# Attention and two gated layers on one core: merging the key halves of the last 64 queries later, a TensorE turn for the first rows, and moved conversions

## The chip, the core and the metric

The kernel runs on one core of one Trainium2 chip. The metric is the time of one execution on the device in microseconds; three executions of the kernel before took 1224.55 to 1224.67, median 1224.65. The profile is of one more execution, and it gives times from the first to the last instruction of that one (its span).

## What is computed

```python
# attention: 4 batches x 8 heads, 1152 keys, head size 64
q_pool = q.reshape(B, H, S // 2, 2, D).mean(axis=3)       # 576 queries
scores = scale * matmul(q_pool, k.T)
scores = scores - max(scores, axis=-1)                     # row maximum
attn = exp(scores); attn = attn / (sum(attn, -1) + 1e-9)
x = attn @ v                      # laid out as 2304 tokens x 512
# two layers, each: h = x @ w_in (512x2048); g = gate(h); x = g @ w_out
# gates: h - tanh(h), then h * sigmoid(1.702 h)
```

## The kernel before, in words

**Attention.** Two heads make a pair; there are 16 pairs, and the two heads of a pair lie in partitions 0 to 63 and 64 to 127 ("sides"). Each pair has two stages, h = 2p and 2p + 1, one for each half of its 576 queries (288 each); so h runs from 0 to 31. A stage computes nine key blocks of scores, transposed (128 keys in the partitions, 288 queries along the free axis): `scores` (L348) issues four steps of two matmuls into one PSUM tile, three for the product in split precision (L355, L356) and a last one, `sel` by `row` (L356), that adds the negated row maximum. ScalarE takes the exponential (L362); POOL adds up key blocks for the row sums (L373). At the stage's end `products` (L381) multiplies by v (L388), sums by ones (L397), and ScalarE copies the result out (L405; L411 for the last pair, tiles `u` and `us`).

**Row maxima** have to be known before the scores of their stage. `unit(p, n)` (L289) computes a piece of the untransposed scores into a PSUM tile `mx` and reduces it on VectorE (L316) into two columns of `mt`. Units 0 to 5 are three 128-query blocks by two 512-key blocks, unit 6 is the last 128 keys for four query blocks, 7 and 8 are the fourth query block. Units 9 and 10, the corners, are the last 64 queries (QL): their matmuls (L311) put the first half of the keys' scores in partitions 0 to 63 and the second half's in 64 to 127, so that one reduction handles both. `max_rows` (L318) merges columns of `mt`: part 0 for the first 384 queries (L324), part 1 for the rest; part 1 also merges the corner's two chunks (L327) and, with a `tensor_tensor` that reads partitions 64 to 127 beside 0 to 63, its two key halves (L328). `send_rows` (L331) transposes 32 by 32 blocks on VectorE (L335) and writes the pieces into `row` with small DMAs (L342), on SP's queue (SPq).

**Order.** Everything is scheduled by hand. All tiles of the attention in PSUM (`mx`, `sc`, `acc`, `warm`) share four buffers in turn; a tile's first matmul waits until the reader of the tile four before is done. The strings `usual` and `begin` (L457, L458) give each stage's order: S is a block of scores, X, C and R are units (own units 7 to 10 or 9 and 10 first, then units of the next pair). A usual even stage does units 9 and 10 of its own pair and 0 to 3 of the next; a usual odd stage does 4 to 8. Part 1 is merged and sent right after unit 10, inside the even stage; part 0 after unit 6, inside the odd stage (L570 to L575). Around the products, jobs are run at four places: "start", "load", "pre" and "gp" (ahead of the products in program order) and "end" (behind them). An engine runs its instructions strictly in this order, so a "pre" job on ScalarE comes behind the last exponential and before the copy of `acc`, and an "end" job behind that copy.

Such jobs are: the preparation of later pairs (L258 to L287, `ql` at L274 on VectorE, `kl` at L287 on POOL), the normalisation of the pair before (`sums`, `recip`, `spread`, `normalise`, L413 to L446), the first eight pieces of the weights (`piece`, L169: a load on SP, then shift, sign, flush, tail and split, L127 to L156, on ScalarE, VectorE and POOL), and `split_x` (L103) of the first token block: a ScalarE copy (L106) and a VectorE subtraction (L107) for each of four heads' pairs. The pieces take one step per stage from h = 2 (`slots_at`, L479) and the rest in h = 30 and 31; `split_x` runs at the "end" of h = 20, 22, 24 and 26 (L489).

**The opening** (L512 to L553): loads, then units 0 to 6 of pair 0 with idle matmuls (`keep_warm`, L514, L517) between them, `max_rows` and `send_rows` of part 0 (three of the six DMAs on ScalarE's queue), 15 pairs of idle matmuls, and then stage 0.

**The layers** (`moe`, L587) follow: 40 jobs of two steps, each the first product (L613, two PSUM tiles `h`), the gate on ScalarE, VectorE and POOL, and two steps later the second product (L708, four PSUM tiles `y`). Its PSUM and SBUF pools are laid where the attention's were. The first token block was split in the attention; the second is split at its first "start" (L755 to L758), ahead of the first gate in ScalarE's order.

## Time and profile before

| | |
|---|---|
| median of three runs | 1224.65 us (1224.55 to 1224.67) |
| the profiled execution's own time | 1224.87 us |
| its span, first to last instruction | 1223.1 us |
| TensorE matmuls (PE) busy | 1199.9 us, 98% |
| weight loads (PEld) busy | 980.5 us, 80% |
| VectorE (DVE) busy | 903.2 us, 74% |
| ScalarE (ACT) busy | 623.0 us, 51% |
| GpSimd (POOL) busy | 481.4 us, 39% |
| granted TensorE clock | 1.000 of full speed (2.4 GHz) |
| attention, up to the first matmul of the layers | 423.24 us |

The attention fills the first third of the span and the layers the rest. Matmuls overlap and their ends are modelled, so that the shares of PE tell little by themselves: what a stage costs is read from the distance between the starts of its products and those of the stage before. A chain of waits is followed back from the end of its stretch: every piece in it either released the next one or stood right ahead of it on its engine. Square brackets in a row of the timeline give the idle time of the engine before the row and what ended it.

### The profile page before, as it was taken

The numbers are of one execution on the slowest core, as the hardware profiler recorded it, in microseconds if no ns is written. First come the engines' busy times: TensorE is split into PE (matmuls) and PEld (weight loads), VectorE is DVE, ScalarE is ACT, GpSimd is POOL, SyncE is SP. The second block draws the span as 40 slices with busy tenths as digits, with TensorE's granted clock in tenths as the row PEclk, the third lists the DMA queues.
The fourth block names the chain that finished last, engine by engine and source line by source line (L and its number), as shares of the span: only waits on it lengthen the run. The fifth ranks groups of instructions, "written<-read, shape, count | busy, mean of one in ns | idle before, by whom it ended". The sixth has DMA issues, their size and how long they took to land.

```text
span 1223.1 us, 23096 instructions
## 1 busy us (share of the span) xinstructions
PE 1199.9 (98%) x9484; PEld 980.5 (80%) x9484; DVE 903.2 (74%) x1053; ACT 623.0 (51%) x914; POOL 481.4 (39%) x325
## 2 busy tenths in 40 slices
PE   9999999999999999999999999999999999999998
PEld 7777767676667787898898898898888888888887
DVE  6688887887678599999999999999545645554333
ACT  3565656565455487666656656656433222322211
POOL 5687887877777523333233323232100101100000
PEclk9999999999999999999999999999999999999999
DMA  3322232223321111111101011111111111110011
GB/s 122 117 75 87 91 125 97 84 74 102 113 87 41 30 45 35 53 52 53 35 35 53 35 50 38 35 43 61 52 36 52 35 52 35 52 35 18 27 59 71
DMA packets 30506, 73.09 MB, mean 60 GB/s; under 512 B 11200, under 2 KB 11712, under 8 KB 30400
## 3 DMA queue, kind: packets, MB, share of 16 engines
q1 hardware_dynamic: 30376, 71.61, 17.1%
q8 instruction: 74, 1.21, 0.4%
q14 instruction: 32, 0.26, 0.1%
q10 hardware_dynamic: 24, 0.00, 0.0%
HBM read 66.58 MB, written 4.79 MB: 58 GB/s over the span
## 4 chain that ended last, share of the span: by engine, by line
PE 73%; DVE 17%; ACT 6%; issue 2%; POOL 2%; DMA 0%; SPq 0%; DVEq 0%; POOLq 0%; ACTq 0%
PE y L708 24%; PE h L613 22%; PE acc L388 11%; PE sc L359 9%; DVE mt L316 4%; PE acc L397 3%; PE mx L304 3%; DVE gg L671 2%; DVE gg L654 2%; ACT u L652 2%; DVE wt L134 2%; ACT a L673 1%; DVE xb L728 1%; DVE m L328 1%; DVE wt L128 1%
## 5 line engine op out<-in xcount | busy, mean ns | idle before, releaser
L316 DVE TENSOR_REDUCE mt<-mx 128x2 fp32r<-128x1024 f32 (+2 forms) x176 | 194.8, 1133 | 69.0 <-PE mx L304 44.4
L613 PE MATMUL h<-hl,big 128*128 128x512 f32 (+1 forms) x940 | 211.6, 377 | 0.0
L156 POOL TENSOR_TENSOR big<-wt,big 128x512 fp32r<-128x512 f32 x46 | 61.0, 1327 | 364.7 <-ACT big L155 364.7
L613 PEld LDWEIGHTS h<-hl,big 128*128 128x128 f32 x940 | 174.0, 188 | 28.6
L362 ACT ACTIVATE pf<-sc 128x576 f32<-128x576 f32 x288 | 173.9, 653 | 42.4 <-PE sc L359 32.8
L373 POOL TENSOR_TENSOR sum<-sum,pf 128x576 f32<-128x576 f32 x126 | 183.7, 1458 | 9.9
L708 PE MATMUL y<-g,big 128*128 128x512 f32 (+1 forms) x780 | 185.3, 368 | 0.7 <-POOL g L625 0.6
L708 PE MATMUL y<-big,g 128*128 128x512 f32 x702 | 181.0, 390 | 0.0
L708 PEld LDWEIGHTS y<-g,big 128*128 128x128 f32 x780 | 142.7, 188 | 20.7 <-POOL g L625 2.3
L708 PEld LDWEIGHTS y<-big,g 128*128 128x128 f32 x702 | 131.6, 188 | 27.1
L623 ACT ACTIVATE g<-gg 128x1024 fp32r<-128x1024 f32 (+1 forms) x80 | 77.9, 974 | 137.9 <-DVE gg L684 78.2
L388 PE MATMUL acc<-pf,v 128*32 128x288 f32 x2304 | 146.3, 407 | 0.3 <-DVE mt L316 0.3
L728 DVE TENSOR_TENSOR xb<-xb,y 128x512 f32<-128x512 f32 (+1 forms) x114 | 72.2, 655 | 86.8 <-PE y L708 86.8
L613 PE MATMUL h<-hl,w 128*128 128x512 f32 (+1 forms) x564 | 127.0, 377 | 0.9 <-ACT e L667 0.9
L388 PEld LDWEIGHTS acc<-pf,v 128*32 128x32 f32 x2304 | 71.6, 110 | 65.9 <-ACT pf L362 4.3
L613 PEld LDWEIGHTS h<-hl,w 128*128 128x128 f32 x564 | 104.3, 188 | 18.3 <-ACT e L667 1.2
L625 POOL TENSOR_TENSOR g<-gg,g 128x1024 fp32r<-128x1024 f32 (+1 forms) x39 | 87.3, 2238 | 62.0 <-ACT g L623 62.0
L673 ACT ACTIVATE a<-u 128x1024 f32<-128x1024 f32 (+1 forms) x40 | 39.1, 977 | 131.7 <-DVE gg L671 131.7
L680 ACT ACTIVATE a<-h 128x1024 f32<-128x1024 f32 (+1 forms) x40 | 37.6, 941 | 117.4 <-PE h L613 117.4
L359 PE MATMUL sc<-qh,kh 64*128 64x288 f32 x576 | 91.5, 314 | 4.3 <-DVE mt L316 4.3
L359 PE MATMUL sc<-row,sel 64*128 64x288 f32 x576 | 85.3, 291 | 0.4 <-DMA row<-tt 0.4
L625 DVE TENSOR_TENSOR g<-gg,g 128x1024 fp32r<-128x1024 f32 (+1 forms) x41 | 48.9, 1193 | 49.6 <-ACT g L623 49.6
(91 smaller groups left out, 2051.7 us busy)
## 6 DMA issues: line engine op xcount, KB each, us to landing
raw<-in_moe_w_in_dram SPq DMA_DIRECT2D x32, 512.0 KB
raw<-in_moe_w_out_dram SPq DMA_DIRECT2D x32, 512.0 KB
v<-in_v_dram SPq DMA_DIRECT2D x16, 576.0 KB
kr<-in_k_dram SPq DMA_DIRECT2D x15, 576.0 KB
qr<-in_q_dram SPq DMA_DIRECT2D x15, 576.0 KB
rbd<-rd SPq DMA_DIRECT2D x32, 144.0 KB
out_dram<-xb SPq DMA_DIRECT2D x18, 256.0 KB
row<-tt SPq DMA_DIRECT2D x125, 0.5 KB
```

The source lines that it names most:

```text
L156: nc.gpsimd.tensor_tensor(lo, t, f32(hi), op=ALU.subtract)
L316: nc.vector.tensor_reduce(out, src, AX.X, ALU.max, negate=True)
L359: nc.tensor.matmul(sc[:, s, 0:HB], w[r], m[r, xs], start=(n == 0), stop=(n == 3))
L362: nc.scalar.activation(pf, sc[:, :, 0:HB], AF.Exp, scale=SCALE)
L373: nc.gpsimd.tensor_add(out, parts[p, x], new)
L388: nc.tensor.matmul(acc[32 * n:32 * n + 32, 0], pairs[p]["v"][:, s, t, 32 * h:32 * h + 32], new[t][:, s, :], start=(t == 0), stop=(t == KT ...
L613: nc.tensor.matmul(hb[:, j, 0:TBS[b]], wi[:, c, w, :], x[r][c], start=(k == 0), stop=(k == 3 * NKC - 1))
L623: nc.scalar.activation(gt[:, :, 0, :], g, AF.Copy)
L625: eng.tensor_tensor(gt[:, :, 1, :], g, f32(gt[:, :, 0, :]), op=ALU.subtract)
L673: nc.scalar.activation(a, u, AF.Relu, bias=-T2)
L708: nc.tensor.matmul(ys[m][:, 0:w], lhsT, rhs, start=(fp == 0 and not low and j == p == 0), stop=(fp == 1 and low and j == 1))
L728: nc.vector.tensor_add(dst, dst, ys[m][:, 0:w])
```

## The change

Corners: the corner units write into columns of `mt` beside the others, so that one reduction makes the four results of part 1, and L327 and L328 go. The two key halves, which lie in different partitions, are no longer merged there: all 128 values of a side are sent, into a new tile `cr`, and a VectorE reduction `end_rows` over the two halves writes the last 64 columns of `row`, behind the products of the even stage in program order and ahead of its "end" jobs. Part 0 of pair 0 no longer goes through transposes and DMAs: `first_rows` turns it with six small matmuls against an identity, and one ScalarE copy writes `row`. Before it, the first three steps of stage 0's first two score blocks are issued; 4 pairs of idle matmuls stand in place of 15. The orders of the first two stages change: one unit (index 2 of pair 1) goes from stage 0 to stage 1. The steps of the weights' pieces are all done by h = 30 with their last split at the "pre" of h = 31; h = 20, 24 and 28 take two steps each. `split_x` goes to the "pre" of h = 10, 12, 14 and 16. `us` is put in a pool that outlives the attention, and `y`'s PSUM pool is made before `h`'s.

```diff
         nil = fixed("nil", 128)
         sel = ap.tile([128, 128], F32R, name="sel")
...
-        mts = [[fixed(f"{nm}{i}", 32) for nm in ("mt", "m2", "m3")] for i in range(2)]
+        m2, ident = spare[0][:, 0:384], spare[1][:, 0:64]
+        nc.vector.memset(f32(m2), 0.0)
+        mts = [[fixed(f"{nm}{i}", 32) for nm in ("mt", "m3")] for i in range(2)]
+        crs = [ap.tile([128, 2 * QL], F32R, name=f"cr{i}") for i in range(2)]
...
+            nc.gpsimd.memset(f32(ident), 0.0)
+            for r in sides:
+                nc.gpsimd.affine_select(
+                    out=ident[r], in_=f32(ident[r]), compare_op=ALU.not_equal, fill=1.0, base=0,
+                    pattern=[[-1, 64]], channel_multiplier=1)
+            for mt, _ in mts:
+                nc.gpsimd.memset(f32(mt[:, 28:30]), 3.0e38)
...
-            for t in rows:
+            for t in rows + crs:
                 nc.gpsimd.memset(f32(t[:]), 0.0)
...
         def new_pair(p):
-            mt, m2, m3 = mts[p % 2]
-            pairs[p] = dict(mt=mt, m2=m2, m3=m3, cq=corners[p % 2], row=rows[p % 2], twos=[])
+            mt, m3 = mts[p % 2]
+            pairs[p] = dict(mt=mt, m3=m3, cq=corners[p % 2], row=rows[p % 2],
+                cr=crs[p % 2], twos=[])
...
-                out = d["mt"][:, 16:24].rearrange("p (j s) -> p j s", j=4)
+                out = d["mt"][:, 20:28].rearrange("p (j s) -> p j s", j=4)
...
-                out, src = d["mt"][:, 8 * c + 2 * j:8 * c + 2 * j + 2], mx
+                out, src = d["mt"][:, 10 * c + 2 * j:10 * c + 2 * j + 2], mx
...
-                out, src = d["mt"][:, 24 + 2 * a:26 + 2 * a], mx[:, :, 0:HB]
+                out, src = d["mt"][:, 8 + 10 * a:10 + 10 * a], mx[:, :, 0:HB]
             nc.vector.tensor_reduce(out, src, AX.X, ALU.max, negate=True)
 
-        def max_rows(p, part):
+        def max_rows(p, part, out=None):
             d = pairs[p]
-            n = 6 if part == 0 else 2
-            at = 0 if part == 0 else 6
-            m = d["m2"] if part == 0 else d["m3"]
-            mt = f32(d["mt"][:, 0:24]).rearrange("p (c j) -> p j c", c=3)
-            nc.vector.tensor_reduce(m[:, 0:n], mt[:, at:at + n, :], AX.X, ALU.min)
-            if part == 1:
-                c = f32(d["mt"][:, 24:28]).rearrange("p (a s) -> p s a", a=2)
-                nc.vector.tensor_reduce(m[:, 2:4], c, AX.X, ALU.min)
-                nc.vector.tensor_tensor(
-                    m[0:64, 2:4], f32(m[0:64, 2:4]), f32(m[64:128, 2:4]), op=ALU.min)
+            mt = f32(d["mt"][:, 0:30]).rearrange("p (c j) -> p j c", c=3)
+            at, n = (0, 6) if part == 0 else (6, 4)
+            out = d["m3"][:, at:at + n] if out is None else out
+            nc.vector.tensor_reduce(out, mt[:, at:at + n, :], AX.X, ALU.min)
...
         def send_rows(p, part):
             d = pairs[p]
-            m = d["m2"] if part == 0 else d["m3"]
             tt = ap.tile([128, 32], F32R, tag="tt", name="tt", bufs=2)
-            nc.vector.transpose(f32(tt[:]), f32(m[:]))
-            for c in range(6 - 2 * part):
+            nc.vector.transpose(f32(tt[:]), f32(d["m3"][:]))
+            for c in range(6 * part, 6 + 4 * part):
                 j, s = divmod(c, 2)
-                q0 = 384 * part + 128 * j
-                w = min(128, SP - q0)
-                row = f32(d["row"][64 * s:64 * s + 1, q0:q0 + w])
-                queue = nc.scalar if p == part == 0 and c % 2 else nc.sync
-                queue.dma_start(
-                    out=row.rearrange("o (a i) -> o a i", i=32),
-                    in_=f32(tt[c:c + 32 * (w // 32 - 1) + 1:32, :]))
+                row = f32((d["row"] if j < 4 else d["cr"])[:])
+                q0 = 128 * j if j < 4 else 0
+                nc.sync.dma_start(
+                    out=row[64 * s:64 * s + 1, q0:q0 + 128].rearrange("o (a i) -> o a i", i=32),
+                    in_=f32(tt[c:c + 97:32, :]))
+
+        def end_rows(p):
+            d = pairs[p]
+            nc.vector.tensor_reduce(
+                d["row"][:, 512:], f32(d["cr"][:]).rearrange("p (h i) -> p i h", h=2),
+                AX.X, ALU.min)
+
+        def first_rows():
+            max_rows(0, 0, m2[:, ::64])
+            rp = ps.tile([128, 2, 512], F32, tag="ps", name="rp")
+            for j in range(3):
+                for a, r in enumerate(sides):
+                    nc.tensor.matmul(
+                        rp[:, a, 64 * j:64 * j + 64], m2[r, 128 * j:128 * j + 128], ident[r],
+                        start=True, stop=True)
+            nc.scalar.activation(
+                pairs[0]["row"][:, 0:384].rearrange("p (j a i) -> p a j i", j=3, a=2),
+                rp[:, :, 0:192].rearrange("p a (j i) -> p a j i", j=3), AF.Copy)
...
-        def scores(g):
+        opened = {}
+
+        def scores(g, some=slice(0, 4)):
             p, i = divmod(g, 2 * KT)
             x, t = divmod(i, KT)
             d = pairs[p]
-            sc = ps.tile([128, 2, 512], F32, tag="ps", name="sc")
+            sc = opened.pop(g, None)
+            if sc is None:
+                sc = ps.tile([128, 2, 512], F32, tag="ps", name="sc")
+            else:
+                some = slice(3, 4)
             ks, xs = slice(128 * t, 128 * t + 128), slice(HB * x, HB * x + HB)
             steps = (
                 (d["kh"][:, ks], d["qh"]), (d["kl"][:, ks], d["qh"]),
                 (d["kh"][:, ks], d["ql"]), (sel, d["row"]))
-            for n, (w, m) in enumerate(steps):
+            for n, (w, m) in list(enumerate(steps))[some]:
                 for s, r in enumerate(sides):
                     nc.tensor.matmul(
                         sc[:, s, 0:HB], w[r], m[r, xs], start=(n == 0), stop=(n == 3))
+            if some.stop < 4:
+                opened[g] = sc
+                return
             pf = ap.tile([128, 2, HB], F32, tag="pf", name="pf", bufs=10)
             nc.scalar.activation(pf, sc[:, :, 0:HB], AF.Exp, scale=SCALE)
             probs[g] = pf
...
-                        wpool.tile([128, SP], F32, name="u"), ap.tile([128, SP], F32, name="us"))
+                        wpool.tile([128, SP], F32, name="u"), wpool.tile([128, SP], F32, name="us"))
...
         usual = "S C S C S S X S S S X S S X X", "S X S S S X S R S S S X S X"
-        begin = "S X S X S C S C S S S S X S X X", "S X S X S X S R S S S S X S X"
+        begin = "S X S S S X S C S S S C S X X", "S X S S S X S S X S X S S R X X"
...
-        slots_at = [h for h in range(2, NH) for _ in range(1 if h < NH - 2 else 3)]
+        slots_at = [h for h in range(2, NH - 1) for _ in range(2 if h in (20, 24, 28) else 1)]
         for n, (kind, f) in enumerate(order):
             ld, shift, *more, split = piece(kind, f)
             mine = slots_at[4 * n:4 * n + 4]
             at(mine[0], "pre", shift)
             for h, job in zip(mine[1:], more, strict=True):
                 at(h, "end", job)
-            at(min(mine[-1] + 1, NH - 1), "pre" if mine[-1] < NH - 1 else "end", split)
+            at(mine[-1] + 1, "pre", split)
         for c in range(NKC):
-            at(NH - 12 + 2 * c, "end", split_x, 0, [c], nc.vector)
+            at(10 + 2 * c, "pre", split_x, 0, [c], nc.vector)
...
-        warm = [ps.tile([128, 2, 512], F32, tag="ps", name="warm") for _ in range(3)][-1]
+        warm = ps.tile([128, 2, 512], F32, tag="ps", name="warm")
...
         for n in range(7):
             unit(0, n)
             keep_warm(4)
-        max_rows(0, 0)
-        send_rows(0, 0)
-        keep_warm(15)
+        for g in range(2):
+            scores(g, slice(0, 3))
+        keep_warm(2)
+        first_rows()
+        keep_warm(2)
...
             products(p, x)
+            if x == 0:
+                end_rows(p)
             do(h, "end")
...
         mp = ctx.enter_context(tc.tile_pool(name="moe", bufs=1))
+        ps_y = ctx.enter_context(tc.tile_pool(name="ps_y", bufs=4, space=PSUM))
         ps_h = ctx.enter_context(tc.tile_pool(name="ps_h", bufs=2, space=PSUM))
-        ps_y = ctx.enter_context(tc.tile_pool(name="ps_y", bufs=4, space=PSUM))
```

## Rows read from the trace of the kernel before

**Rows 1.** Stages: us; busy PE, PEld, DVE, ACT, POOL; clock, DMA share, GB/s

```profile
239.62:252.68 13.06, 12.45 (x180) 8.84 (x184) 11.34 (x14) 8.31 (x15) 10.05 (x8) 1.00 0.17 46
252.68:264.65 11.97, 11.97 (x180) 8.78 (x184) 8.96 (x12) 6.89 (x14) 10.84 (x8) 1.00 0.46 172
277.71:290.90 13.19, 12.13 (x180) 8.74 (x184) 8.90 (x13) 5.93 (x13) 10.47 (x8) 1.00 0.45 157
...
560.00:1100.00 540.00, 538.27 (x2538) 465.54 (x2537) 407.92 (x473) 263.74 (x342) 115.41 (x70) 1.00 0.12 43
```

**Rows 2.** Chain of waits, stages 18 to 21: start us, us, what

```profile
247.74 0.14 DVE m L327
...
247.90 1.06 DVE m L328
...
250.36 0.50 PE mx L304 x2
250.86 1.06 PE sc L359 x16
...
260.71 0.23 PE mx L304 x2
...
283.90 0.42 ACT big L106
```

**Rows 3.** VectorE's lines L328, L335, L274: duration in ns, least, median, most

```profile
L328 DVE TENSOR_TENSOR m<-m x16: 246/1054/1059, 23.7 to 403.0; 64x2 fp32r<-64x2 f32 x16
...
L335 DVE STREAM_TRANSPOSE tt<-m x32: 211/211/214, 15.2 to 404.1; 128x32 f32<-128x32 f32 x32
...
L274 DVE TENSOR_TENSOR ql<-qs,qh x15: 697/1499/1960, 28.4 to 385.8; 128x576 fp32r<-128x576 f32 x15
```

**Rows 4.** Timeline of POOL, stage 18

```profile
247.51 1.43 POOL L373 TENSOR_TENSOR sum<-pf 128x576 f32<-128x576 f32 x1 [2.62 <-ACT pf L362]
```

**Rows 5.** Timeline of TensorE, stages 18 and 19

```profile
247.81 0.39 PE L304 MATMUL mx<-kh,qh 64*128 64x512 f32 x2
...
249.49 0.29 PE L359 MATMUL sc<-row,sel 64*128 64x288 f32 x2
...
258.71 0.40 PE L304 MATMUL mx<-kh,qh 64*128 64x512 f32 x2
```

**Rows 6.** Timeline of VectorE, stages 18 and 19

```profile
254.47 0.77 DVE L128 TENSOR_SCALAR wt<-raw 128x512 int32<-128x512 int32 x1
...
259.16 1.23 DVE L316 TENSOR_REDUCE mt<-mx 128x2 fp32r<-128x1024 f32 x1 [2.16 <-PE mx L304]
```

**Rows 7.** Chain of waits, the opening and stages 0 and 1

```profile
14.99 0.18 DVE m L324
...
16.87 1.70 DMA row<-tt
...
18.71 0.70 PE sc L359 x2
...
26.28 4.57 PE acc L388 x72
...
39.30 4.50 PE acc L388 x72
```

**Rows 8.** Timeline of SP's queue, stage 1 (six of L342)

```profile
38.03 3.22 SPq L342 DMA_DIRECT2D row<-tt  x6
```

**Rows 9.** Timeline of TensorE, stages 30 and 31 and the layers' first steps

```profile
410.77 0.43 PE L397 MATMUL acc<-sum,ones 128*32 128x288 f32 x1 [0.61 <-POOL sum L373]
...
423.24 4.45 PE L613 MATMUL h<-big,w 128*128 128x384 f32 x24 [0.83 <-ACT us L411]
...
432.72 5.70 PE L613 MATMUL h<-hl,w 128*128 128x512 f32 x24 [0.86 <-ACT e L667]
```

**Rows 10.** Chain of waits where the layers begin

```profile
425.02 1.86 DMA s<-us
...
427.07 2.20 ACT hl L106 x4
```

## The prediction

> **What bounds the kernel now.** I read the table of stages first. From 560 to 1100 us PE is busy for 538.27 of 540 us at clock 1.00 [rows 1]: the layers run at TensorE's pace, so what the attention or the turn to the layers gains moves the layers forward as a block and reaches the end. In the attention a usual even stage takes 13.06 us and the odd one behind it 11.97, though PE is never idle in the odd one and the even one has nearly the same work, two corner units in place of unit 6 [rows 1]. The same 13.06 stands in all 14 even stages from 2 to 28; the odd stages 21, 23, 25 and 27 take 13.19 instead of 11.97, of which PE sits idle for 1.06 [rows 1].
>
> The chain of waits says why. In the even stage it leaves PE, goes through VectorE's merging of the corners (L327 0.14 us, L328 1.06) and comes back to PE at 250.36, when a reduction has freed a PSUM buffer [rows 2]. PE's last matmul ahead of that starts at 249.49 and takes 0.13 to the next, so PE stood from 249.62 to 250.36 [rows 2, 5]. L328 works on 64 by 2 values, and its least time is 246 ns, its median 1054 [rows 3]. It begins at 247.90 and ends at 248.96; POOL's addition runs from 247.51 to 248.94 [rows 2, 4]. So most of L328 is a wait for POOL's instruction to end.
>
> In the slow odd stages the chain goes through ScalarE's `split_x` copy, which stands between the copy of `acc` and the next exponentials [rows 2].
>
> **The change, part by part.** Durations and the sum are those of the profiled execution: 1224.87 us, 1223.1 of it span, 0.22 above the median of the runs.
>
> *Corners, even stages 2 to 28.* L327 and L328 go: 0.14 + 1.06 and two hand-overs of 0.02 to 0.04, about 1.25 us on VectorE ahead of the transpose. The following reduction is then limited by its matmul: TensorE issues it at 247.81, and in the odd stage such a reduction starts 0.45 after its matmul (258.71 to 259.16) and takes 1.23, so the buffer is free at 247.81 + 0.45 + 1.23 = 249.49 [rows 5, 6]. PE wants it at 249.62: that wait goes. Late next is the last unit's buffer: freed at 249.62 + 0.45 + 1.23 = 251.30, wanted, after two units of 0.23 and 1.06 of scores, at 251.14 [rows 2]. A wait of 0.16 stays, and a restart (0.50 for a unit's two matmuls behind a wait, in place of 0.23 [rows 2]): products at 251.80 instead of 252.68, 0.88 earlier. Without that wait, with a unit's 0.39 [rows 5], it is 251.14 + 0.39 = 251.53, 1.15 earlier. The bounds are these two. I take 0.95, near the replay with the wait, since its two times are only 0.16 apart: 14 x 0.95 = **13.3 us**.
>
> *What takes their place.* `end_rows` is a reduction of 128 by 128 values: between L327 (4 values, 0.14) and a unit (1024, 1.23) that is about 0.27 [rows 2, 6]. It lies behind the units on VectorE, where 2.16 us are idle before the next stage's first reduction [rows 6]; its cost is nothing while that holds, 0.27 a stage if it doesn't. It adds a wait for four DMAs. The transpose is done at about 248.0, SP issues four DMAs at 3.22 / 6 = 0.54 each, and the last lands 1.70 later, at 251.9 [rows 7, 8]. VectorE comes to it after its last unit and L128, at some 254. Behind it stand `recip`, `ql` and the next stage's reductions, with that same idle time. The corners' DMAs are four as before, 128 values each for 64.
>
> *`split_x`* leaves the "end" of stages 20 to 26: 4 x (13.19 - 11.97) = **4.9 us**. At the "pre" of 10 to 16 ScalarE's copy (0.42) lies in the products' 4.5 us, when ScalarE waits for `acc`. The subtraction is a VectorE instruction with two inputs; `ql` of that kind takes 0.70 to 1.96 here [rows 3], and POOL is busy beside it. I take nothing: its cover is the 2.16 us, and without that an odd stage would lose what it loses now. The Trainium skill (SBUF — State Buffer, Who interferes with whom) says that a VectorE instruction with two SBUF inputs and a GpSimd one that reads SBUF exclude each other for a whole instruction, while a reduction never contends. L328 agrees with it. By that rule the moved subtraction can block, or be blocked, each time: it is the third rival below.
>
> *Weights' steps.* From 30 and 31 they go to 20, 24 and 28, a second VectorE step each, of 0.70 to 1.96 by the nearest kind of row [rows 3], in the same idle time: nothing, or at worst 3 x 0.9 where the stage already has `ql` and a shift. The pieces' loads come up to two stages earlier on SP, past loads of q, k and v; each needs a buffer whose last reader runs three stages before, so SP isn't held. In stage 30 PE waits 0.61 for POOL's sums [rows 9], which ran against three of these steps on VectorE: **0.6 us**, or nothing.
>
> *The opening.* Part 0's reduction ends at 15.17 and the first `row` step starts at 18.71 [rows 7]: 3.54 us of transpose, DMA issue and 1.70 of landing. New: six 64-column matmuls, at most three pairs of 0.39 [rows 5], I take 0.4; PE's queue ahead of them (two opened blocks, two idle pairs) ends, as I put it, near 15.6; a ScalarE copy of 384 columns, 0.42 as L106 [rows 2], with hand-overs: `row` is there at 16.6, 2.1 earlier. From there the old stage took 26.28 - 18.71 = 7.57 to its products. It now has six steps of scores less and one unit less, and VectorE's reductions are spread. PE's work is seven blocks of 0.53, two last steps and six units of 0.23 to 0.27, some 5.5 us [rows 2]; with small waits for buffers I take 5.9. First products at 22.5 in place of 26.28: **3.8 us**, bounds 2.1 (the row alone) and 4.3. POOL's new constants and VectorE's memset fall where both wait for the first loads. The granted clock is 1.000 over the whole span, the present pauses of the opening included, and the new ones (about 0.2 us ahead of the `row` step) are shorter; so 22 idle matmuls less cost nothing.
>
> *Stage 1* now holds seven units: 11.97 + 0.23 and the usual small waits, 12.4, against 13.02 [rows 7]: 0.6 less. But unit 6 comes late, so the transpose ends 1.1 after the products start; six DMAs (3.22) and 1.70 of landing [rows 7, 8] make it 6.05 after, and stage 2 wants `row` at 5.9: 0.3 lost with the restart. **0.3 us**, bounds -1 and +1.
>
> *The turn.* `split_x` of the second block starts on ScalarE at 427.07, behind the DMA that reads `us` (425.02 + 1.86); the first gate follows it, and the third product begins at 432.72 after 0.86 of idle PE [rows 9, 10]. With `us` out of the attention's memory and the last split gone from ScalarE's queue, the copies start near 423.2 and end at 425.4, before the first product does (about 427.6, where its 4.45 end). The gate then starts when the first product ends, near 427.6, instead of 429.27, and releases the third product 1.7 earlier, at 431.0; PE is ready at 432.72 - 0.86 = 431.86: **0.9 us**. The order of the PSUM pools could save the 0.83 ahead of the first product too [rows 9]; the trace doesn't show which buffer the last `acc` holds, so that is only in the bounds.
>
> **Sum:** 13.3 + 4.9 + 0.6 + 3.8 + 0.3 + 0.9 = 23.8 us off 1224.87: **1201.1 us**.
>
> **Rivals.** *(1) Backlog on VectorE.* The even stages become shorter and VectorE keeps `end_rows`, `ql` and the conversions in a smaller gap, so that the odd stage gives half back. Against it: the 0.27 of `end_rows` and the 0.3 by which the reductions end later against the products leave 1.6 of the 2.16 us. For it: `ql`'s spread to 1.96. 14 x 0.5 returned: 1208. *(2) POOL too late.* It is busy for 10.05 + 10.84 of the 25.03 us of a pair [rows 1], of 24.1 then, and its additions must fall between the exponentials and the ones-matmuls. If 0.3 a pair is lost: 1205.3. *(3) `split_x` costs the same where it is put*, if the moved subtraction waits for POOL's instruction as L328 does, or POOL for it: 4.9 back, 1206. *(4) The opening stays bound by VectorE's reductions*, with only the row's 2.1 gained or less: 1203.5. *(5) The wait moves on*: the transpose meets POOL's instruction in L328's place, and the 13.3 us go: 1214.5. Against it: 32 transposes of 211 to 214 ns, whatever POOL did [rows 3]. *(6) Slower.* `end_rows` waits for its DMAs at the head of VectorE's queue and every even stage's reductions behind it stand. To lose the 23.8 us, 15 stages must each lose 1.6 beyond the idle time: the DMAs would have to land at about 259.7, 9 us after their issue, not 1.70. Price from there: each further microsecond costs 15 us, 1240 at one.
>
> **Chances.** The forecast 0.54; (1) 0.13, (2) 0.08, (3) 0.07, (4) 0.08, (5) 0.05, (6) 0.03, and 0.02 for a gain within 0.2%, which is about what a measurement here tells from no change. Low end: the bounds (0.2 more in each of 14 stages, 0.8 at the first product, 0.5 at the opening, 0.7 in stage 1) together give 1196.3. High end: 1209 takes in (1) to (4). Faster 0.95, same 0.02, slower 0.03.
>
> **What would show it.** Right: even stages of about 12.1, odd ones of 12.0 throughout, no VectorE instruction of the corner chain above 0.25 us, first products near 22.5, the third product of the layers right behind the second, the layers' own length unchanged. Wrong: PE waiting in odd stages for a reduction (1) or for POOL in the ones-matmuls (2); stages 11 to 17 longer than 12 (3); idle VectorE before `end_rows`, released by a DMA (6). The forecast falls as a whole if even stages stay at 13.06 with L328 gone.

## The result, and the profile after

The changed kernel takes 1205.66 us, the median of four runs (1205.05 to 1205.94), beside 1224.60 for the kernel before: a ratio of 0.9845 [0.9828, 0.9862]. That is 18.9 us, where 23.5 were forecast from the median; the time lies inside the range. The profiled execution took 1205.63 us, 1203.8 of it span, at a clock of 1.00.

The table of stages of the changed kernel shows stages 16 to 19, and a stretch of the layers (us; busy PE, PEld, DVE, ACT, POOL; clock, DMA share, GB/s):

```profile
205.70:217.92 12.22, 12.19 (x179) 8.80 (x177) 10.37 (x12) 8.32 (x15) 9.28 (x7) 1.00 0.04 4
217.92:230.84 12.92, 12.25 (x178) 8.81 (x176) 12.08 (x14) 6.18 (x13) 10.89 (x9) 1.00 0.43 161
230.84:243.07 12.23, 12.20 (x179) 8.80 (x177) 9.72 (x12) 8.32 (x15) 8.30 (x6) 1.00 0.18 47
243.07:255.06 11.99, 11.99 (x179) 8.80 (x177) 9.79 (x13) 6.87 (x14) 11.62 (x9) 1.00 0.49 174
541.90:1081.90 540.00, 538.16 (x2538) 465.52 (x2537) 408.10 (x472) 263.75 (x342) 115.50 (x70) 1.00 0.13 43
```

Against [rows 1] the even stages went from 13.06 to 12.22 or 12.23, with PE idle for 0.03 of that by the modelled ends of its matmuls, and the layers run as before. Stage 17, the second row, takes 12.92 instead of 11.98, with PE idle for 0.67. TensorE's timeline of stage 18 shows a wait that is left in the even stages:

```profile
240.91 0.40 PE L315 MATMUL mx<-kh,qh 64*128 64x512 f32 x2
241.16 0.29 PE L385 MATMUL sc<-qh,kh 64*128 64x288 f32 x2
...
242.21 0.93 PE L315 MATMUL mx<-kh,qh 64*128 64x512 f32 x4
243.07 4.57 PE L417 MATMUL acc<-pf,v 128*32 128x288 f32 x72
```

A unit in the middle of the stage takes 0.25 to the start of the next matmul (240.91 to 241.16); the last two take 0.86 to the products, as in the kernel before (0.84). The chain of waits has the last unit start at 242.64, 0.43 behind the one ahead of it, when a VectorE reduction frees its buffer. Matmuls overlap, so the idle time hides most of this.

VectorE's timeline shows the end of stage 16, the part of stage 17 ahead of PE's idle 0.67, and stage 30:

```profile
213.85 0.17 DVE L334 TENSOR_REDUCE m<-mt 128x4 fp32r<-128x12 f32 x1
214.06 0.21 DVE L339 STREAM_TRANSPOSE tt<-m 128x32 f32<-128x32 f32 x1
...
219.77 1.74 DVE L107 TENSOR_TENSOR big<-xb,big 128x384 fp32r<-128x384 f32 x1
221.43 0.28 DVE L350 TENSOR_REDUCE row<-cr 128x64 fp32r<-128x128 f32 x1
221.63 1.71 DVE L141 SCALAR_TENSOR_TENSOR wt<-wa,wt 128x512 f32<-128x512 f32 x1
...
223.60 1.91 DVE L285 TENSOR_TENSOR ql<-qs,qh 128x576 fp32r<-128x576 f32 x1
225.43 1.21 DVE L327 TENSOR_REDUCE mt<-mx 128x2 fp32r<-128x1024 f32 x1
...
388.95 0.29 DVE L350 TENSOR_REDUCE row<-cr 128x64 fp32r<-128x128 f32 x1 [3.45 <-DMA cr<-tt]
```

POOL's timeline over the same stretch of stages 16 and 17:

```profile
216.68 4.42 POOL L402 TENSOR_TENSOR sum<-sum,pf 128x576 f32<-128x576 f32 x3
221.05 1.74 POOL L298 TENSOR_TENSOR kl<-kr,kh 128x576 fp32r<-128x576 f32 x1
223.45 1.44 POOL L274 TENSOR_TENSOR qs<-qr 128x576 f32<-128x576 f32 x1 [0.66 <-DVE r L455]
```

Merge and transpose now follow each other directly; the 1.06 of [rows 2] is gone. But `split_x`'s subtraction (L107) takes 1.74 us, and it ends 0.41 after POOL's `sum` (219.77 + 1.74 = 221.51; 221.10). The flush behind it (L141) takes 1.71 and ends 0.55 after POOL's `kl` (223.34; 222.79). `ql` takes 1.91. Then the next stage's first reduction starts late, and PE waits.

The chain of waits of the opening stands against [rows 7]:

```profile
13.74 1.44 POOL qs L274
...
15.20 0.68 ACT qh L278
15.89 0.39 ACT row L362
...
16.32 0.40 PE sc L385 x2
...
22.40 4.50 PE acc L417 x72
```

The `row` step starts at 16.32 instead of 18.71, and stage 0's products at 22.33 (the first record of them; the chain has 22.40) instead of 26.28. The copy of `row` stood behind `qh` of pair 1 on ScalarE, which waits for POOL's `qs`; by the trace the turning matmuls were done at 15.44.

TensorE's timeline at the end of stage 30 and in the turn, against [rows 9]:

```profile
392.66 0.43 PE L426 MATMUL acc<-sum,ones 128*32 128x288 f32 x1 [0.44 <-POOL sum L402]
...
405.13 4.43 PE L646 MATMUL h<-big,w 128*128 128x384 f32 x24 [0.83 <-ACT us L440]
409.40 4.32 PE L646 MATMUL h<-big 128*128 128x384 f32 x24
413.56 5.64 PE L646 MATMUL h<-hl,w 128*128 128x512 f32 x24
```

The third product comes right behind the second, 8.43 after the first instead of 9.48. The wait of 0.83 ahead of the first is as it was.

### The profile page after: what moved, and what is told of

Same layout as the page of the kernel before. It is cut to its first block, busy times and chain, and to the rows that moved or that the text cites. A ratio compares the mean times of both kernels' runs of the same rounds, so it can differ in the third digit from the quotient of the medians.

```text
span 1203.8 us, 23024 instructions
## 1 busy us (share of the span) xinstructions
PE 1192.8 (99%) x9468; PEld 977.5 (81%) x9468; DVE 910.0 (76%) x1035; ACT 623.9 (52%) x915; POOL 484.2 (40%) x332
## 3 DMA queue, kind: packets, MB, share of 16 engines
q8 instruction: 74, 1.21, 0.4%
## 4 chain that ended last, share of the span: by engine, by line
PE 73%; DVE 16%; ACT 7%; POOL 2%; issue 2%; DMA 1%; DVEq 0%; SPq 0%; ACTq 0%; POOLq 0%
PE y L741 23%; PE h L646 22%; PE sc L385 13%; PE acc L417 10%; DVE gg L704 3%; PE mx L315 3%; PE acc L426 2%; DVE gg L687 2%; ACT u L685 2%; DVE wt L134 2%; ACT a L706 2%; DVE wt L141 1%; DVE wt L128 1%; DVE xb L761 1%; DVE wt L148 1%
## 5 line engine op out<-in xcount | busy, mean ns | idle before, releaser
L327 DVE TENSOR_REDUCE mt<-mx 128x2 fp32r<-128x1024 f32 (+2 forms) x176 | 195.6, 1136 | 54.2 <-PE mx L315 30.5
```

Of the source, the lines that this page charges most:

```text
L327: nc.vector.tensor_reduce(out, src, AX.X, ALU.max, negate=True)
```

## The experiments

The experiments are called e1 to e12. Every kernel changes the one after, except e3, which changes the one before. Ratios are to the kernel before. Unless said otherwise each computes everything.

**The corners' merge put back (e1).**

```diff
+            if part == 1:
+                m = d["m3"]
+                nc.vector.tensor_tensor(
+                    m[0:64, 8:10], f32(m[0:64, 8:10]), f32(m[64:128, 8:10]), op=ALU.min)
...
-                row = f32((d["row"] if j < 4 else d["cr"])[:])
...
-            if x == 0:
-                end_rows(p)
```

> The changed kernel with the merge of the corners' two key halves put back between the reduction and the transpose (64 by 2 values, two inputs); cr and end_rows go, all else stays. Theory (that instruction waits for POOL's first addition to end, holds the reductions behind it, and so the PSUM buffers): it takes 1.05 us in the even stages 2 to 28, these take 12.9 to 13.1 us again instead of 12.23, and the kernel 1205.7 + 14 x 0.8 = 1216 to 1218. Rival (the gain comes from elsewhere, L327 or the corners' column order): it takes 0.25, the even stages stay within 0.2 of 12.23, 1206 to 1208.

1214.11 us, 0.9914 [0.9899, 0.9929]. The merge instruction (least, median, most ns), and a usual even stage in the table of stages:

```profile
L337 DVE TENSOR_TENSOR m<-m x16: 158/1043/1047, 22.6 to 394.1; 64x2 fp32r<-64x2 f32 x16
```

```profile
235.51:248.56 13.05, 12.44 (x178) 8.83 (x176) 11.27 (x13) 8.30 (x15) 10.01 (x8) 1.00 0.17 45
```

The even stages are back at 13.05 to 13.06. The loss is less than 14 of their gains, because the odd stages from 11 to 17 went to 11.97 to 12.03 and stage 29 to 11.98: beside longer even stages the late `ql` harms nothing, though `split_x`'s subtraction still takes 0.89 to 1.63.

**`split_x` in stage 31 (e2).**

```diff
-            at(10 + 2 * c, "pre", split_x, 0, [c], nc.vector)
+            at(NH - 1, "pre", split_x, 0, [c], nc.vector)
```

> The changed kernel with all four split_x steps of the first block at the pre of stage 31 instead of one each at 10, 12, 14 and 16. Theory (in stages 10 to 16 the moved subtraction and the steps behind it wait for POOL's instructions on VectorE and hold the next stage's first reduction): stages 11, 13, 15 and 17 go from 12.24, 12.65, 12.24 and 12.92 to 12.0, 2.1 us in all, and stage 31 has room on ScalarE (4 x 0.42 in the products' 4.5 us) and VectorE: 1203.5. Rival (those odd stages are long for another reason, such as the conversions' steps there): they stay long, 1205.5 or, with a later turn, more.

1204.08 us, 0.9833 [0.9818, 0.9847], 1.6 under the changed kernel. Stages 11, 13, 15 and 17 take 11.97 to 11.99. The subtraction of `split_x` (first four of eight in the attention), in the changed kernel:

```profile
L107 DVE TENSOR_TENSOR big<-xb,big x8: 542/1096/1741, 147.5 to 774.1; 128x384 fp32r<-128x384 f32 x8
```

and with all four in stage 31:

```profile
L107 DVE TENSOR_TENSOR big<-xb,big x8: 545/554/1637, 399.7 to 772.4; 128x384 fp32r<-128x384 f32 x8
```

It is 0.55 alone and up to 1.74 beside POOL. Stage 22 was 0.63 too long in this execution, so that not all of the 2.1 shows.

**POOL's additions one block later, in the kernel before (e3).** The sum starts with blocks 1 and 2 and takes block 0 last (pairs 1 to 14); nothing else is changed.

```diff
-            new = probs[(2 * p + x) * KT + t]
-            if t == 0:
-                parts[p, x] = new
...
+            if t < 2:
+                return
+            blocks = [probs[(2 * p + x) * KT + i] for i in range(t + 1)]
+            if t == 2:
+                parts[p, x] = ap.tile([128, 2, HB], F32, tag="sum", name="sum")
+                nc.gpsimd.tensor_add(parts[p, x], blocks[1], blocks[2])
+                return
+            nc.gpsimd.tensor_add(parts[p, x], parts[p, x], blocks[t])
+            if t == KADD - 1:
+                nc.gpsimd.tensor_add(parts[p, x], parts[p, x], blocks[0])
```

> The kernel before with one thing changed: for pairs 1 to 14 POOL's five additions of a stage start with blocks 1 and 2 and take block 0 last, so that the first one begins about 0.65 us later, behind the third exponential instead of the second. The number of additions is the same. Theory (L328 is long only because it meets POOL's first addition): it takes 0.25 us where it took 1.05, the even stages 4 to 28 fall from 13.06 to about 12.3, and the kernel from 1224.6 to 1214 to 1216, the merge still in its place. Rival (L328 is long by itself, or it meets some other instruction of POOL): it stays at 1.05 and the kernel at 1224 or above.

1221.75 us, 0.9977 [0.9967, 0.9986]. The old merge instruction:

```profile
L328 DVE TENSOR_TENSOR m<-m x16: 156/156/1016, 23.5 to 399.5; 64x2 fp32r<-64x2 f32 x16
```

The table of stages, 22 and 23:

```profile
282.85:295.07 12.22, 12.18 (x179) 8.80 (x177) 9.86 (x14) 8.31 (x15) 7.49 (x6) 1.00 0.14 45
295.07:312.09 17.02, 13.69 (x178) 10.30 (x176) 11.10 (x13) 7.19 (x15) 13.95 (x10) 0.90 0.35 123
```

VectorE's timeline in stage 23:

```profile
301.77 1.79 DVE L107 TENSOR_TENSOR big<-xb,big 128x384 fp32r<-128x384 f32 x1 [3.92 <-ACT big L106]
...
303.83 1.76 DVE L274 TENSOR_TENSOR ql<-qs,qh 128x576 fp32r<-128x576 f32 x1
305.51 2.34 DVE L316 TENSOR_REDUCE mt<-mx 128x2 fp32r<-128x1024 f32 x2
```

TensorE's timeline at the same place:

```profile
302.88 0.29 PE L359 MATMUL sc<-row,sel 64*128 64x288 f32 x2
...
306.77 0.47 PE L359 MATMUL sc<-qh,kh 64*128 64x288 f32 x2 [3.33 <-DVE mt L316]
307.04 0.44 PE L359 MATMUL sc<-qh,kl 64*128 64x288 f32 x2
```

The merge of the same two operands falls to 156 ns, and the even stages to 12.22 to 12.28, with all the corner instructions in place: L328's microsecond was POOL's, and one block of delay takes it away. Most of the gain didn't reach the end, because `split_x` still stood at the "end" of 20 to 26. VectorE waits there for ScalarE's copy, with `ql` and the reductions behind it. In stage 23 of the kernel before, the subtraction and `ql` took 0.56 and 0.70, mostly while POOL was idle; here they run beside POOL's `qs` and first addition and take 1.79 and 1.76. Stages 21 and 25 take 13.44 and 13.43, 23 and 27 take 17.02 and 16.97. In stage 23 PE stood for 3.33 us; behind that the granted clock was 0.50 (1.2 GHz) from 308 to 310 us, 0.90 over the stage, and the same pairs of matmuls took 0.44 instead of 0.29.

**A unit of the next pair one place earlier in the even stage (e4).**

```diff
-        usual = "S C S C S S X S S S X S S X X", "S X S S S X S R S S S X S X"
+        usual = "S C S C S S X S S X S S S X X", "S X S S S X S R S S S X S X"
```

> The changed kernel with one score block moved in the usual even stage, from between the first and second of the next pair's units to behind the second: S C S C S S X S S X S S S X X. Theory (what keeps even stages at 12.23 is the last unit's wait for the buffer of the second, 0.05 to 0.16, and the restart behind it, 0.27; with the second unit 0.53 earlier its buffer is free in time): even stages of 11.9 to 12.0, 14 x 0.27 = 3.8 less, 1202. Rival (VectorE's reductions are the bound and the wait moves to the second unit or the next stage): 12.2 or more, 1205.5 to 1207.

1205.56 us, 0.9843 [0.9827, 0.9860]; an even stage in the table of stages:

```profile
230.90:243.09 12.19, 12.16 (x178) 8.71 (x176) 9.50 (x12) 7.97 (x14) 8.36 (x6) 1.00 0.17 46
```

Nothing is gained, because the wait has moved. TensorE's timeline of that stage, at the second unit of the next pair:

```profile
240.44 0.40 PE L315 MATMUL mx<-kh,qh 64*128 64x512 f32 x2
240.87 0.40 PE L385 MATMUL sc<-qh,kh 64*128 64x288 f32 x2
```

The last two units now take 0.55 to the products instead of 0.86, but the score block behind the second unit starts 0.43 after it instead of 0.25, again when a VectorE reduction ends. This is what the rival said, with the wait at a score block.

**The opening put back (e5).** Part 0 of pair 0 goes through transposes and six DMAs, three on ScalarE's queue; 15 idle pairs.

```diff
+                queue = nc.scalar if p == part == 0 and c % 2 else nc.sync
+                queue.dma_start(
...
-        for g in range(2):
-            scores(g, slice(0, 3))
-        keep_warm(2)
-        first_rows()
-        keep_warm(2)
+        max_rows(0, 0)
+        send_rows(0, 0)
+        keep_warm(15)
```

> The changed kernel with the opening's rows sent by transpose and six DMAs again (three on ScalarE's queue), stage 0's first blocks not opened ahead, and 15 pairs of idle matmuls; the new order of stages 0 and 1 stays. Theory (the row step sets the start of stage 0, the rest of the gain is the new order and the opened blocks): the row step near 18.7 instead of 16.6, first products near 24.4 instead of 22.33, and 2.1 us more: 1207.7. Rival (VectorE's reductions set the first products): within 0.7 of 22.33, 1205.7 to 1206.4.

1207.55 us, 0.9859 [0.9844, 0.9874]. The second side's first `row` step in TensorE's timeline:

```profile
18.77 0.37 PE L386 MATMUL sc<-row,sel 64*128 64x288 f32 x1 [0.48 <-DMA row<-tt]
```

It is back at 18.77 and the products start at 25.04, 2.7 later than in the changed kernel (24.4 was expected). The kernel is only 1.9 slower, mostly because stage 17 took 11.98 here instead of 12.92: `ql` started 0.2 ahead of POOL's `qs` and took 0.70 instead of 1.91. The products are still 1.2 ahead of 26.28. That is most likely the unit that left stage 0: with the corners' old path (e1) they start at 22.41, much as in the changed kernel.

**The order of the PSUM pools put back (e6)**, `h`'s before `y`'s.

> The changed kernel with h's PSUM pool made before y's again. The changed kernel's first product still waits 0.83 us for the copy of us, as before. Theory (the order of the pools changes nothing, the first tile of the layers waits for all readers of the attention's PSUM): 1205.7 within the noise, the same wait of 0.83. Rival (the order saves something later, when y's tiles are first written): 1206 to 1207.

1205.94 us, 0.9844 [0.9830, 0.9859], and the first product of the layers waits 0.83 as before: this part does nothing here.

**`us` back in the attention's pool (e7).**

```diff
-                        wpool.tile([128, SP], F32, name="u"), wpool.tile([128, SP], F32, name="us"))
+                        wpool.tile([128, SP], F32, name="u"), ap.tile([128, SP], F32, name="us"))
```

> The changed kernel with us in the attention's own pool again. Theory (the copies of the second block's split wait for the DMA that reads us): ScalarE's copies start 3.4 us behind the copy of us instead of 0.3 ahead of its end, the first gate ends later and the third product comes 9.9 to 10.3 us behind the start of the last copy instead of 9.2: 0.7 to 1.1 us more, 1206.4 to 1206.8. Rival (the last split's absence from ScalarE's queue was what counted): 1205.7, the same.

1207.03 us, 0.9856 [0.9841, 0.9870]. The third product in TensorE's timeline:

```profile
415.25 5.70 PE L646 MATMUL h<-hl,w 128*128 128x512 f32 x24 [0.94 <-ACT e L700]
```

It starts 9.56 behind the first product instead of 8.43: this part is worth 1.1 us at the third product.

**A candidate (e8):** `split_x` in stage 31, one piece's load a stage earlier, and in stage 30 two additions on VectorE in place of POOL's later ones.

```diff
-            at(mine[0] - 1, "load", ld)
+            at(mine[0] - 1 - (n == 5), "load", ld)
...
-            at(10 + 2 * c, "pre", split_x, 0, [c], nc.vector)
+            at(NH - 1, "pre", split_x, 0, [c], nc.vector)
...
-                    if h < NH - 1 and t < KADD or t < 4:
+                    if h < NH - 2 and t < KADD or t < 4:
                         add(p, x, t)
-                    elif h == NH - 1 and t in (5, 7):
+                    elif h >= NH - 2 and t in (5, 7):
                         add_two(p, x, t)
```

> The changed kernel with split_x of the first block at the pre of stage 31 (as in e2_splitx_last, 1204.1), one piece's load moved from stage 20 to 19, and in stage 30 two of POOL's five additions replaced by two of VectorE's, as stage 31 has them. Theory (stage 22 was 12.85 in e2_splitx_last because that load stood ahead of q's and POOL's additions came late; stage 30 waits for POOL's additions): stage 22 at 12.2, 0.6 less, and stage 31's products 0.4 to 0.6 earlier: 1203.0 to 1203.2. Rival (POOL is late for another reason, and in stage 30 the wait goes to VectorE): 1204.

1204.94 us, 0.9840 [0.9823, 0.9856]: no better than `split_x` in stage 31 alone. The stretch to the last products fell from 10.99 to 10.46, but stage 21 took 12.76, and the span ended 5.3 behind the start of the last matmul instead of 4.4 in e2. In this kernel, in the changed one and in those of e2 and e4 to e7, the profiled execution has one of stages 21, 22, 25 and 26 long by 0.2 to 0.8. For e2's stage 22 POOL's timeline shows why:

```profile
273.18 1.43 POOL L274 TENSOR_TENSOR qs<-qr 128x576 f32<-128x576 f32 x1 [2.95 <-DMA qr<-in_q_dram]
276.08 6.09 POOL L402 TENSOR_TENSOR sum<-sum,pf 128x576 f32<-128x576 f32 x4
```

POOL waited 2.95 for a load of q, its sums ended at 282.17, and TensorE's ones-matmuls start at 282.22 behind them, after 0.42 of idle time.

**Reductions in place of subtractions (e9).** Stages 10 to 16 keep ScalarE's copy and get, where the subtraction stood, a VectorE reduction of the same 128 by 384 values whose result nothing uses; the subtractions go to stage 31.

```diff
+            nc.vector.tensor_reduce(seen[:, c:c + 1], xb[0][:, c], AX.X, ALU.max)
...
-            at(10 + 2 * c, "pre", split_x, 0, [c], nc.vector)
+            at(10 + 2 * c, "pre", x_high, c)
+            at(NH - 1, "pre", x_low, c)
```

> The changed kernel with split_x's ScalarE copies at 10, 12, 14 and 16 as they are, but VectorE's subtraction there replaced by a reduction over the same 384 columns (one input, of about the same own length, 0.55 us); the four subtractions run at the pre of stage 31. Theory (the long stages 11 to 17 come from two-input instructions waiting for POOL's, 1.3 us for the subtraction alone in stage 16): the reduction takes about 0.55 wherever POOL is, stages 11 and 15 fall to 12.0, 13 and 17 to 12.0 to 12.3; the sum over the four at least 1.5 below the changed kernel's 2.1 excess, 1204 to 1204.5. Rival (VectorE simply has too much to do there): these stages stay at 12.24, 12.65, 12.24 and 12.9, 1205.7.

The odd stages from 11 to 17 take 11.97 to 12.00, and VectorE's lines have the four reductions, as a group:

```profile
L511 DVE TENSOR_REDUCE seen<-xb x4: 537/540/545, 147.6 to 218.7; 128x1 f32<-128x384 f32 x4
```

Where the subtraction took up to 1.74 beside POOL, a reduction of the same shape takes 0.54 every time. That it is the second operand that makes the difference isn't shown, for the reduction also writes one value a partition and the subtraction 384. L128, the shift of the weights' pieces, reads one operand and writes 512 values, and it is lengthened too; in the changed kernel:

```profile
L128 DVE TENSOR_SCALAR wt<-raw x64: 410/745/2518, 49.1 to 1111.3; 128x512 int32<-128x512 int32 x64
```

It takes 0.41 to 0.42 where POOL is idle and up to 2.52 beside it.

Yet the kernel took 1214.77 us, 0.9920 [0.9905, 0.9935]: the layers' first product starts at 402.80, 2.3 ahead of the changed kernel's, and the layers then take 809.7 instead of 798.7. The groups of their matmuls by shape (busy us, mean ns), in this kernel:

```profile
L657 PE MATMUL h<-hl,big 128*128 128x512 f32 x720 | 172.8, 395 | 0.0
L657 PE MATMUL h<-hl,big 128*128 128x384 f32 x220 | 43.3, 337 | 0.0
```

and in the changed one:

```profile
L646 PE MATMUL h<-hl,big 128*128 128x512 f32 x720 | 168.4, 389 | 0.0
L646 PE MATMUL h<-hl,big 128*128 128x384 f32 x220 | 43.2, 335 | 0.0
```

The wide matmuls are slower with no wait, the narrow ones are not. The copies stand where the changed kernel has them and the subtractions where e2 has them, and the layers of both take 798.7; what is new are `seen` and its reductions. `seen` moved the layers' tiles in memory by 32 bytes, so placement was the suspect.

**The merge kept, additions later, `split_x` in stage 31 (e10).** The edits of e1, e2 and e3 together, on the changed kernel.

> The merge of the halves on VectorE as in e1_merge_back, no cr and no end_rows, with POOL's additions of pairs 1 to 14 starting with blocks 1 and 2 as in e3_sums_later, and split_x at the pre of stage 31 as in e2_splitx_last. Theory (all that the corners' new way gains is that VectorE doesn't meet POOL's first addition, so a later start of that addition gains the same): even stages 4 to 28 of 12.2, odd ones of 12.0, 1203.5 to 1205. Rival (the merge costs more than its meeting POOL, or the later additions come late for the ones-matmuls): even stages of 12.4 to 12.6, 1206 to 1209.

1202.65 us, 0.9821 [0.9805, 0.9837]. VectorE and POOL in stage 18, from their timelines:

```profile
237.35 0.15 DVE L337 TENSOR_TENSOR m<-m 64x2 fp32r<-64x2 f32 x1
```

```profile
237.79 1.43 POOL L416 TENSOR_TENSOR sum<-pf 128x576 f32<-128x576 f32 x1 [2.89 <-ACT pf L396]
```

Even stages take 12.21 to 12.25 (stage 12 12.44) and odd ones from 3 to 29 11.96 to 12.10, as with the corners' rewrite. The merge is done before POOL starts.

**The best version (e11):** e8's stage 30, conversions at one step a stage up to stage 29 and two in 30 and 31, two heads' pairs of `split_x` in stage 30 and two in 31, and `qh` of pair 1 behind `first_rows`.

```diff
+        slots_at = [h for h in range(2, NH) for _ in range(1 if h < NH - 2 else 2)]
...
+            at(NH - 2 + c // 2, "pre", split_x, 0, [c], nc.vector)
...
-        prep_qh(1)
...
         first_rows()
+        prep_qh(1)
```

> The changed kernel with: split_x two each at the pre of stages 30 and 31; the pieces' steps one per stage up to 29 and two each in 30 and 31 (no second step at 20, 24 and 28); two of POOL's five additions of stage 30 done by VectorE; pair 1's query conversion behind the first rows' copy on ScalarE. Theory: odd stages 11 to 17 at 12.0 (2.1 less than the changed kernel), no long stage among 21 to 26 (0.2 to 0.8 less), stage 29 at 12.0 (0.4), stage 31 begins 0.5 earlier, first products 0.4 earlier: 1202.0 to 1202.5. Rival (the steps in 30 and 31 hold the first product or POOL again): 1203.5 to 1204.5.

1202.27 us, 0.9817 [0.9803, 0.9832], 3.4 under the changed kernel. The stretch from stage 30's products to stage 31's:

```profile
384.73:395.19 10.46, 10.46 (x162) 7.58 (x161) 6.56 (x10) 7.62 (x16) 6.22 (x4) 1.00 0.10 32
```

No stage from 2 to 29 is above 12.23 any more. The first products start at 22.10, 0.2 earlier and not 0.4.

**e9's tile made 64 bytes a partition (e12)** (`[128, 4 * NKC]` instead of `[128, NKC]`), so that the layers' tiles start at multiples of 64 bytes.

> e9_reduce_for_subtract with one difference: the reductions' result tile has 16 columns (64 bytes in a partition) instead of 4 (which took 32), so that all tiles behind it in SBUF, the layers' x and g among them, lie at a multiple of 64 bytes again instead of 32 off. In e9 the stages 11 to 17 fell as the theory said, but the layers took some 10 us longer, their groups of 24 matmuls of 512 columns 5.60 us instead of 5.44, with no wait of PE. Theory (the place of the moving operand in SBUF sets that pace): 5.44 again, the layers 799 us long, and the kernel 1203.7 to 1204.7. Rival (the subtractions' move or anything else in e9 did it): 5.60 and 1214.8 again.

1212.01 us, 0.9896 [0.9880, 0.9913]; the wide matmuls by shape:

```profile
L657 PE MATMUL h<-hl,big 128*128 128x512 f32 x720 | 170.4, 393 | 0.0
```

They are between the two kernels above, though the tiles are aligned again. Up to 812 us the 512-column matmuls of a group mostly start 229 ns apart, from there 230 to 234; in e9 it is 233 or 234 throughout, in the changed kernel mostly 227 to 229. The alignment to 64 bytes alone isn't the cause; what is stays open.

## Why the prediction was right, and where it was off

The direction and the mechanisms of the large parts held; the likeliest figure, 1201.1, was 4.6 too low. That the time lies at the 1206 of rival (3) is in part luck: (3) came for 2.1 of its 4.9 us, and the corners and the conversions missed another 2.5. Six terms against what the stages show (profiled executions, 19.3 us between their spans):

| term | forecast | measured | how |
|---|---|---|---|
| even stages 2 to 28 | 13.3 | 11.6 | 14 x 0.84, less 0.2 in stage 26 |
| `split_x` | 4.9 | 2.7 | 4 x 1.21 gained in 21 to 27, 2.1 lost in 11 to 17 |
| conversions' steps | 0.6 | -0.2 | stage 29 0.4 longer; 30 and 31 0.2 shorter |
| opening | 3.8 | 3.95 | 26.28 to 22.33 |
| stage 1 | 0.3 | 0.2 | 12.95 to 12.72, between the first records of its products and of stage 0's |
| turn | 0.9 | 1.2 | 1.05 at the third product; the layers as a whole 799.86 to 798.67 |

**Corners.** That L328's microsecond was a wait for POOL is shown: e3 and e10 keep the instruction, and it takes about 0.15 once POOL starts later; e1 brings the 13.06 back. The mis-sized step is the choice behind the replay. The replay put a stage at 13.06 - 0.88 = 12.18 with its last wait in place, and the forecast took 0.95, as if part of that wait went too. Measured are 12.22, with the wait whole: the last unit starts 0.43 behind the one ahead of it, not 0.23, and the products 0.43 behind that, not 0.33 as in stage 19. By these distances an estimate for a stage without the wait is 12.22 - 0.20 - 0.10 = 11.92, so the upper bound of 1.15 was about right for that case. When a score block is moved (e4), the wait moves with VectorE's reductions; no run here took it away.

**`end_rows`** cost nothing, as forecast. Its DMAs do arrive late in stages 0 and 30 (VectorE idle for 1.22 and 3.45 ahead of it), and in the other 14 stages VectorE never waits for them; rival (6) did not come.

**`split_x`** is the step that failed: "I take nothing: its cover is the 2.16 us". The third rival came, for 2.1 of its 4.9. The subtraction takes 1.74 instead of 0.55 beside POOL, and the flush and `ql` behind it are lengthened in the same way (1.71 and 1.91, against 0.69 and 0.70 at least), so that the cover is used up by three instructions, not one. By e9 a reduction in the same place costs nothing. Both agree with the rule cited from the Trainium skill (SBUF — State Buffer, Who interferes with whom). I gave that rival 0.07, though L328 had shown the wait. The doubled steps cost 0.4 in stage 29, within the "0.9 at worst": L128, the sign step and `ql` take 1.61, 1.56 and 1.64 there, and with one step a stage (e11) it takes 11.96.

**The conversions' 0.6** in stage 30 did not come: the fourth of POOL's five additions still took 1.98, beside the one VectorE step left there (L148), and PE waits 0.44 instead of 0.61 there. It took e8's move of the additions themselves to shorten that stretch, by 0.5.

**The opening** was right in sum; `row` came at 16.32 for 16.6. What held it was not the turn but `qh` of pair 1 ahead of the copy on ScalarE, which I had not looked at; with `qh` behind the copy (e11) the step starts at 16.07. In the nine other kernels with this opening the first products start at 22.32 to 22.68, so the term is known to some 0.3.

**The turn** was right and, by e7, for the reason given. The order of the PSUM pools does nothing (e6).

What the forecast did not see at all is a cheaper way: the corners' whole rewrite is worth no more than starting POOL's first addition one block later (e10 keeps the merge and takes 1202.65; e2, with the rewrite and otherwise alike, 1204.08; the usual even stage takes 12.22 in both). In the kernel before it did not pay alone, because `split_x` at the "end" then ran beside POOL (e3). The 11.6 us of the even stages, all there in e3, left 3.0 at the end (1224.72 to 1221.75) while that step stayed.

Open: why most of these kernels have one long stage among 21 to 26 in the profiled execution. For e2 it is a late load of q; e1 and e9 to e12 showed none there (12.10 in stage 21 of e10 at most among the odd ones), but each was profiled once.

## What to carry to other kernels

When a tiny instruction takes four times its least duration, look at which instruction of another engine ends with it; then either put another kind of instruction in its place (here a reduction, which never waited) or shift the other engine's start, and try the shift first, since it can be a few lines. A step that is moved costs what its new place costs: count the instructions that would be lengthened there in a row beside POOL, not the idle time alone. And read a stage's waits from the distances between the starts of matmuls: the idle time said 0.03 of 12.22, the starts some 0.3.

## What the runs showed that I had not expected

- A wait of 3.33 us on TensorE cost more than itself: the stage's mean clock was 0.90 (0.50 from 308 to 310 us), the pairs of matmuls behind it took 0.44 instead of 0.29, and the stage grew by 5.0 (17.02 for 11.98, e3).
- The 512-column matmuls of the layers ran 2.6% slower in e9 (172.8 against 168.4) and 1.2% slower in e12, at clock 1.00 and without a wait, while those of 384 columns did not change. Over the layers that is up to 11 us, more than half of what this change gained, and the cause is open.
